# Output stores of 32 partitions joined in pairs to 64 partitions, in the last stage of a two-branch long convolution

## Chip, cores and metric

The kernel runs on one core of one Trainium2 chip. The metric is the device time of one execution in microseconds (us), lower is better. Before the change the median of three runs is 247.13 us (246.75 to 247.59).

## What is computed

The input is a sequence of 2048 positions with 448 channels in bfloat16. Two long convolutions over the positions are taken of it and mixed by a gate, position by position:

```python
g = sigmoid((x * gate_w).sum(-1, keepdims=True))          # x = A_u, (1, 2048, 448)
a = causal_conv(x, K) + x * Dskip      # K[d, l] = Re sum_n C exp(dt * A * l) * dt * B, by FFT
kv = short_conv4(k, shift_k) * v
b = x * (causal_conv(kv, ssm_k) + kv * ssm_D)              # by FFT
return g * a + (1 - g) * b                                # (1, 2048, 448)
```

The result is one array of 2048 x 448 bfloat16, that is 1,835,008 bytes.

## The kernel before, in words

**Layout.** Position t is written as 64 a + b, with a from 0 to 31 and b from 0 to 63, and the channel as 112 g + l, with g from 0 to 3. The work tiles hold (g, a) on the 128 partitions and (b, l) along each partition. The channels are worked through in four quarters H of 28 columns per group g (`NC`, line 25). `PLAN` (line 37) lists the steps: tables of the first convolution's kernel (T), the convolutions themselves (B, b, a, A), and the mixing of finished quarters (m). Each convolution is a chain of matmul stages with an elementwise product between them; their results leave PSUM by copies on VectorE or ScalarE, chosen one by one in `SIDES` (line 45).

**The last step.** The last entry of `PLAN` is the first convolution of quarter 3. Its last part is `end` (line 980). It runs over four pieces, h and k from 0 to 1, and each piece holds four of the sixteen values of y, where b = 16 x + y. For a piece it:

- collects the last matmul stage in a PSUM bank (lines 987 to 992),
- multiplies by the gate and adds the other branch on VectorE (lines 994 to 996),
- moves the data with matmuls in `relay` (line 965) from partitions (g, a) to partitions (x, a), so that all 448 channels of one position stand together,
- copies it with a change of sign into one of two row tiles, `lines[h]` (line 999; the other quarters have been put there already by `mix`, line 1071),
- stores the piece (lines 1000 and 1001).

**The stores.** After a piece is complete, partition 32 x + a of `lines[h]` holds 4 positions of 448 channels, 3584 bytes, which are contiguous in the output. The view `out_rows` (line 957) is the output as [x, a, y, l]; its x step is 16 positions and its a step is 64 positions. Line 1001 issues one transfer for each x: 32 partitions of 3584 bytes, 112 KB. x = 0 and 2 go to the queue of the sync engine (SP), x = 1 and 3 to that of ScalarE (ACT): `dmae` (line 770) lists the two. The four pieces make 16 transfers, and these are all the writes of the output.

**The order.** `Order` (line 132) records every call of the kernel and then issues the calls in the sequence that the string `ORDER` (line 51) gives; each instruction is chained behind the one before it on its engine. All records of the trace therefore carry line 144. The transfers that ScalarE issues stand in its own instruction stream, between its copies. Each transfer adds to one of eight completion counters used in turn, and waits until the transfer before it on the same counter has landed.

Of the kernel before, what the change touches and what calls it, by code (L numbers as in the profile page):

```python
# [110 lines left out]
)  # L111

def after(tc, ins, before):
# [55 lines left out]
def shaped(flat, shape, dtype=bf16, at=0):  # L169
    n = 1  # L170
    for s in shape:
        n *= s
    ap = flat if dtype is flat.dtype else flat.bitcast(dtype)
    ap = ap[:, at:at + n]
    names = "abcde"[:len(shape)]
    return ap.rearrange("p (%s) -> p %s" % (" ".join(names), " ".join(names)), **dict(zip(names, shape))) if len(shape) > 1 else ap
# [524 lines left out]
class Modes:  # L701
# [5 lines left out]
    def across(self, nm, put):  # L707
        for hf in range(2):
            for g in range(4):
                put(hf, g, self.raw[nm][:, g, hf * 128:(hf + 1) * 128])  # L710
# [36 lines left out]
def body(  # L747
# [22 lines left out]
    dmae = [nc.sync, nc.scalar]  # L770
# [143 lines left out]
    for b0 in range(0, 64, 8):  # L914
        pt = places.room()
        for i in range(2):
            for d in (0, -1, 1, -2, 2, -3, 3):
                t0 = b0 + 4 * i + d
                j0, j1 = max(0, -d), min(4, 4 - d)
                for g in range(4):  # L920
                    x = kT[g][:, t0 % 16, 2 + t0 // 16:2 + t0 // 16 + 4 * 31 + 1:4]
# [35 lines left out]
    out_rows = out[0].rearrange("(a x y) l -> x a y l", a=32, x=4)  # L957
    lines = []

    def line(y0):  # L960
        if not lines:
            lines.extend(qt([8, 448]) for _ in range(2))
        return lines[y0 // 8][:, y0 % 8:]

    def relay(o, g, part, first, last):
        for x in range(4):
            nc.tensor.matmul(o[32 * x:32 * x + 32].rearrange("p (y c) -> p y c", c=NC), lhsT=minus[:, 32 * g:32 * g + 32], rhs=part(x),
                             start=first, stop=last, tile_position=(0, 32 * x))

    def laid(t, H):  # L970
        return t.rearrange("p y (g h c) -> p h g y c", g=4, c=NC)[:, H]
# [8 lines left out]
    def end(U, H):  # L980
        across = lambda t, y0, n: t.rearrange("p (x y) c -> p x y c", x=4)[:, :, y0:y0 + n]
        for h in range(2):
            for k in range(2):
                ps, pt = (places.room()[:, 0] for _ in range(2))
                y0 = 8 * h + 4 * k
                b = across(ug[H], y0, 4)
                nc.tensor.matmul(ps[:, 0:448].rearrange("p (x y c) -> p x y c", x=4, c=NC), lhsT=minus[:], rhs=b, start=True, stop=False)
                for i in range(16):
                    for r in range(2):
                        l = 16 * (i // 4) + y0 + i % 4  # L990
                        nc.tensor.matmul(ps[:, i * NC:(i + 1) * NC], lhsT=G[:, l, r].rearrange("p g a -> p (g a)"), rhs=U[:, r, l],
                                         start=False, stop=(r == 1 and i == 15))
                t = shaped(arena["RK"][:], [4, 4, NC], at=448 * (2 * h + k))
                V.tensor_tensor(out=t, in0=ps[:, 0:448].rearrange("p (x y c) -> p x y c", x=4, c=NC),
                                in1=gt[:].rearrange("p (x y) -> p x y", x=4)[:, :, y0:y0 + 4].unsqueeze(3).to_broadcast([P, 4, 4, NC]), op=ALU.mult)
                V.tensor_tensor(out=t, in0=t, in1=b, op=ALU.add)
                for g in range(4):
                    relay(pt[:, 112 * g:112 * g + 112], g, lambda x: t[:, x], g == 0, g == 3)
                evac.minus(laid(line(y0)[:, 0:4], H), pt[:, 0:448].rearrange("p (g y c) -> p g y c", g=4, c=NC))
                for x in range(4):  # L1000
                    dmae[x % 2].dma_start(out_rows[x][:, y0:y0 + 4], lines[h][32 * x:32 * x + 32, 4 * k:4 * k + 4])

    held_open = []

# [50 lines left out]
    def conv_A(what, H, K):  # L1055
        X = spread_in(lambda c: uu[:, :, H * NC + c])
        transform(nc, places, W2, X, evac)
        X, S = swapped(X)
        if H < NQG - 1:
            transform(nc, places, W2, K, evac)  # L1060
            conv(products(nc, X, S, K), what, H)
            return
        U = qt([2, 64, NC])
        for c0 in (0, CB):
            transform(nc, places, W2, K, evac, c0, c0 + CB)
            for k0 in (0, 16):
                products(nc, X, S, K, k0, k0 + 16, c0, c0 + CB)
            stage_a(nc, places, R, whole(U, evac), (X, S), [range(c0, c0 + 8), range(c0 + 8, c0 + CB)])
        end(U, H)
# [57 lines left out]
```

## Time and profile before

| | |
|---|---|
| median of 3 runs | 247.13 us |
| the profiled execution's own time | 248.35 us |
| its span, first to last instruction | 246.4 us |
| busy: TensorE, VectorE, ScalarE | 85%, 93%, 89% of the span |
| bytes written to the device memory, whole run | 2.87 MB |
| first store of the output issued | 236.9 us |

The profile is one execution on the chip. Its span goes from the first instruction to the last; the execution's own time is 1.95 us longer than the span. Engines are PE (TensorE), DVE (VectorE), ACT (ScalarE), POOL (GpSimd) and SP (the sync engine); a name with a small q behind it (SPq, ACTq) is the engine's queue, where transfers are issued. The core has 16 DMA engines that carry out all transfers; the view of the transfers gives their mean busy share and the rate of bytes, and counts packets. In a row of the view by stretches of time stand the stretch, its length, the busy time of each engine with its instruction count, the granted clock of TensorE (PEclk), the busy share of the 16 DMA engines, and GB/s.

### The profile page before, as it was taken

The page shows a single profiled execution, that of the slowest core. Times are in us where ns is not written, and L with a number is a line of the kernel's source. Part 1 is how long each engine was busy: PE and PEld are TensorE (multiplying, and loading weights), DVE is VectorE, ACT ScalarE, POOL GpSimd, SP SyncE. Part 2 cuts the span into 40 slices and gives each one's busy share as a digit, 9 for nine tenths or more (in the row PEclk, how much of TensorE's full clock was granted, in tenths as well). Part 3 has the DMA queues.
Part 4 walks back from the last instruction along what each step waited for, and adds up shares of the span by engine and source line. Part 5 has one row for each costly group of instructions (what it writes and reads, how often), then busy time and mean ns, then how long its engine had stood idle before and what let it go on. Part 6 is the DMA issues. An engine that isn't in the chain of part 4 may idle for free.

```text
span 246.4 us, 12201 instructions
## 1 busy us (share of the span) xinstructions
PE 209.4 (85%) x5451; PEld 185.5 (75%) x5451; DVE 228.4 (93%) x394; ACT 220.4 (89%) x333; POOL 39.9 (16%) x112
## 2 busy tenths in 40 slices
PE   0747699877999998887899988979999999999970
PEld 0645277566988988787889977978989998998850
DVE  7999999999686999999999999999999999989870
ACT  5999999998999999999999999989999997586640
POOL 8700002030002141000011450001434102000000
PEclk9999799999999999999999999999999999999985
DMA  5997999993103498000688680000775402300035
GB/s 131 306 184 155 238 203 192 187 195 79 23 5 78 116 228 168 7 5 3 92 118 152 142 215 24 7 3 11 125 132 155 114 5 68 89 4 3 3 115 186
DMA packets 43347, 26.27 MB, mean 107 GB/s; under 512 B 34144, under 2 KB 40256, under 8 KB 43296
## 3 DMA queue, kind: packets, MB, share of 16 engines
q1 hardware_dynamic: 38848, 15.64, 30.9%
q0 software_dynamic: 3600, 8.95, 18.0%
q8 instruction: 42, 0.69, 1.2%
q10 hardware_dynamic: 848, 0.92, 1.1%
q14 instruction: 9, 0.07, 0.1%
HBM read 9.78 MB, written 2.87 MB: 51 GB/s over the span
## 4 chain that ended last, share of the span: by engine, by line
PE 36%; DVE 23%; ACT 19%; DMA 7%; issue 7%; SPq 4%; POOL 0%; DVEq 0%; ACTq 0%; POOLq 0%
PE ps L144 36%; ACT q L144 15%; DVE TP L144 10%; DVE TQ L144 5%; SPq L144 4%; DVE q L144 4%; ACT G L144 3%; DMA natu<-in_A_u_dram 3%; DMA gw<-in_gate_w_dram 2%; DMA TP<-TP 2%; DMA q<-in_B_ssm_k_dram 1%; DVE RK L144 1%; DVE ET L144 1%; DVE G L144 1%; DVE natv L144 1%
## 5 line engine op out<-in xcount | busy, mean ns | idle before, releaser
L144 ACT CAST q<-ps 128x896 bf16<-128x896 f32 (+4 forms) x172 | 133.2, 900 | 11.1 <-PE ps L144 10.6
L144 PEld LDWEIGHTS <-q 128*128 128x128 bf16 (+2 forms) x784 | 41.0, 134 | 8.9 <-issue 3.8
L144 PEld LDWEIGHTS <-G 128*128 128x128 bf16 (+2 forms) x1136 | 35.5, 103 | 15.3 <-issue 7.2
L144 DVE TENSOR_TENSOR TQ<-TQ,ET 128x896 bf16<-128x896 bf16 (+2 forms) x70 | 45.4, 682 | 0.1
L144 PE MATMUL ps<-q,s_W 128*128 128x112 bf16 (+1 forms) x544 | 33.5, 210 | 3.8 <-ACT q L144 2.1
L144 PE MATMUL ps<-sa_R,q 128*128 128x128 bf16 x448 | 33.6, 229 | 3.3 <-issue 1.7
L144 PE MATMUL ps<-TP,TQ 128*32 128x32 bf16 x1792 | 32.9, 240 | 2.1 <-issue 1.8
L144 PEld LDWEIGHTS <-s_W 128*128 128x128 bf16 x544 | 27.6, 97 | 7.6 <-issue 4.9
L144 PEld LDWEIGHTS <-TQ 128*32 128x32 bf16 x1792 | 29.9, 153 | 4.2 <-issue 2.3
L144 DVE TENSOR_TENSOR q<-q,q 128x3584 bf16<-128x3584 bf16 (+1 forms) x22 | 32.3, 1508 | 0.6 <-ACT q L144 0.6
L144 POOL DMA_DIRECT2D TP<-TP x15 | 13.4, 895 | 112.0 <-PE ps L144 64.8
L144 DVE TENSOR_TENSOR TP<-TP,ET 128x1792 bf16<-128x1792 bf16 (+3 forms) x25 | 31.5, 1269 | 0.1
L144 ACT ACTIVATE q<-hold 128x224 bf16<-128x224 f32 (+1 forms) x81 | 28.7, 410 | 0.1
L144 POOL DMA_DIRECT2D q<-q x30 | 16.1, 564 | 56.2 <-ACT q L144 30.2
L144 PEld LDWEIGHTS <-natu 128*64 128x64 bf16 (+1 forms) x288 | 21.5, 206 | 4.8 <-DMA natu<-in_B_k_dram 3.6
L144 PE MATMUL ps<-q,G 128*128 128x56 bf16 (+1 forms) x640 | 20.3, 182 | 1.0 <-ACT q L144 0.9
L144 ACT ACTIVATE ET<-q 128x1344 bf16<-128x1344 int16 (+1 forms) x12 | 17.3, 1477 | 0.0
L144 PE MATMUL ps<-Wc,natu 128*64 128x128 bf16 x224 | 16.5, 284 | 0.5 <-ACT q L144 0.5
L144 PE MATMUL ps<-Wc,natv 128*64 128x128 bf16 x224 | 16.1, 285 | 0.6 <-ACT q L144 0.6
L144 PEld LDWEIGHTS <-natv 128*64 128x64 bf16 x224 | 15.2, 213 | 1.5 <-issue 1.0
L144 DVE TENSOR_TENSOR TQ<-TQ 128x448 bf16<-128x448 bf16 (+2 forms) x35 | 15.3, 443 | 0.2
L144 PE MATMUL ps<-G 112*32 112x336 bf16 (+3 forms) x448 | 14.0, 274 | 1.3 <-issue 0.7
(96 smaller groups left out, 280.0 us busy)
## 6 DMA issues: line engine op xcount, KB each, us to landing
TP<-TP POOLq DMA_DIRECT2D x9, 448.0 KB, 5.8
q<-q SPq DMA_DIRECT2D x34, 112.0 KB, 3.4
q<-q POOLq DMA_DIRECT2D x30, 112.0 KB, 4.0
natu<-in_B_k_dram SPq DMA_DIRECT2D x2, 896.0 KB, 10.3
q<-in_B_ssm_k_dram SPq DMA_DIRECT2D x16, 112.0 KB, 3.8
natv<-in_B_v_dram SPq DMA_DIRECT2D x8, 224.0 KB, 5.3
natu<-in_A_u_dram SPq DMA_DIRECT2D x8, 224.0 KB, 8.1
TP<-TP POOLq DMA_DIRECT2D x6, 224.0 KB, 3.6
```

What stands on the lines that cost most here:

```text
L144: ins = f(*args, **kw)
```

## The change

In each piece, the four stores of 32 partitions become two of 64 partitions: x = 0 and 1 go in one transfer on SP's queue, x = 2 and 3 in one on ScalarE's. On the side of the output the transfer runs over 2 values of x, 32 values of a, and 1792 contiguous elements; on the side of the row tile it runs over 64 partitions and 1792 contiguous elements. The bytes, their places, and the instructions of PE, DVE and POOL stay as they are. The rest of the diff renumbers the calls in the string `ORDER`, since eight calls are gone; the order of the others is kept.

```diff
-                for x in range(4):
-                    dmae[x % 2].dma_start(out_rows[x][:, y0:y0 + 4], lines[h][32 * x:32 * x + 32, 4 * k:4 * k + 4])
+                for x in (0, 2):
+                    dmae[x // 2].dma_start(out_rows[x:x + 2, :, y0:y0 + 4], lines[h][32 * x:32 * x + 64, 4 * k:4 * k + 4])
```

In the built programs the instructions of the two queues differ only here (each line is output and source, and the extent of the output side):

```
SP   before: out<-q 32x1792   eight times      after: out<-q 2x32x1792   four times
ACT  before: out<-q 32x1792   eight times      after: out<-q 2x32x1792   four times
```

6 rows, old and new, of the table ORDER are left out of this document.

## Prediction

> **What bounds the kernel now.** The change touches only the stores of the output, so I read the end of the run: first the page's chain and its row of slices, then the view by stretches of time, the list of the queues' issues, and the transfers of the last 14.4 us.
>
> The chain of work that ended last, its final pieces (start, duration, what):
>
> ```profile
> 225.96 11.64 PE ps L144 x293
> ...
> 238.28 0.40 DVE RK L144
> 238.69 0.04 issue
> 238.73 0.89 PE ps L144 x28
> 239.62 0.02 issue
> 239.64 0.62 DVE q L144
> ```
>
> The last copy, on DVE, ends at 239.64 + 0.62 = 240.26 us. The span is 246.4 us (page, first line, below), so after the last computation about 6.1 us pass with nothing left but stores. What happens in them, by stretches:
>
> ```profile
> span 246.4 us, 12201 instructions
> ```
>
> ```profile
> 10.00:12.00 2.00, 1.34 (x15) 1.34 (x16) 2.00 (x10) 2.00 (x4) 1.38 (x14) 1.00 1.02 415
> 237.70:244.70 7.00, 0.86 (x32) 0.58 (x32) 1.86 (x4) 0.73 (x2) 0.00 (x0) 0.60 0.86 262
> 238.00:244.00 6.00, 0.86 (x32) 0.58 (x32) 1.56 (x4) 0.54 (x1) 0.00 (x0) 0.59 0.92 282
> 240.00:241.00 1.00, 0.00 (x0) 0.00 (x0) 0.26 (x1) 0.00 (x0) 0.00 (x0) 0.50 0.90 291
> 241.00:242.00 1.00, 0.00 (x0) 0.00 (x0) 0.00 (x0) 0.00 (x0) 0.00 (x0) 0.50 0.88 269
> 242.00:243.00 1.00, 0.00 (x0) 0.00 (x0) 0.00 (x0) 0.00 (x0) 0.00 (x0) 0.50 0.89 269
> 243.00:244.00 1.00, 0.00 (x0) 0.00 (x0) 0.00 (x0) 0.00 (x0) 0.00 (x0) 0.50 0.95 298
> 244.70:246.40 1.70, 0.00 (x0) 0.00 (x0) 0.00 (x0) 0.00 (x0) 0.00 (x0) 0.50 0.00 0
> ```
>
> The two columns to read are the last ones, the busy share of the 16 DMA engines and GB/s. From 238 to 244 us the engines are 92% busy at 282 GB/s; PE, DVE and ACT end in the meantime. After 244.7 us nothing moves, and 1.7 us later the span is over: that is the last completion and the program's end. **So the tail is bound by the DMA engines**, and they are what this change rearranges. The first row, from the loads at the start, is kept as the fastest rate of this trace: 415 GB/s with all engines busy.
>
> The stores themselves, as the trace lists them (count, issue times in ns, first and last start), and their queues in the stretch from 232 us on:
>
> ```profile
> L144 SPq DMA_DIRECT2D out_dram<-q x8: 315/362/558, 236.9 to 241.5; - x8
> L144 ACTq DMA_DIRECT2D out_dram<-q x8: 321/408/773, 236.9 to 242.1; - x8
> ```
>
> ```profile
> q1 hardware_dynamic: 384, 0.92, 23.9%
> q10 hardware_dynamic: 384, 0.92, 17.9%
> ...
> out_dram<-q SPq DMA_DIRECT2D x8, 112.0 KB, 3.0
> out_dram<-q ACTq DMA_DIRECT2D x8, 112.0 KB, 3.1
> ```
>
> q1 is SP's queue, q10 ACT's. Each queue's 8 stores have 8 x 32 = 256 rows of 3584 bytes, yet 384 packets: 16 more for each store. I read these as one completion packet from each of 16 engines, so each store of before lies on all 16, two rows on each. The packets took (0.239 + 0.179) x 16 engines x 14.4 us = 96.3 us, or 188 ns a row.
>
> **The change, part by part.**
>
> Removed: eight issues, four on SP and four on ACT, of 0.36 and 0.41 us. All issues of before are out by 242.1 + 0.77 = 242.9 us while the engines have work until 244.7, so fewer issues save at most the gaps of the engines, priced under the first rival. Removed too is a wait on reused completion counters: eight stores now have eight counters. In the waits of SP's queue it is small:
>
> ```profile
> SPq L144 <- DMA out_dram<-q: 0.4, 2, 0.2
> ```
>
> It lies under the full engines; I count it at nothing, and 0.4 us if that cover were gone.
>
> Moved: nothing. The programs stand in the same order on PE, DVE and POOL, and the eight remaining stores in the same places behind the same copies.
>
> Added: two kinds of thing, a longer issue and **another division over the DMA engines**.
>
> *Issue.* A store's description is longer. The nearest rows are SP's other 64-partition transfers and a transfer with only four rows (times in ns, as above):
>
> ```profile
> L144 SPq DMA_DIRECT2D q<-q x5: 461/548/1214, 202.8 to 209.2; - x5
> L144 SPq DMA_DIRECT2D d<-in_A_Dskip_dram x1: 864/864/864, 24.2 to 24.2; - x1
> ```
>
> I take 0.55 us, from the first of them because it too has 64 partitions: 0.2 us more than 0.362, which counts once, ahead of the first data. The ends are no change and 0.864 - 0.362 = 0.5 us. On ACT the copies stand behind the stores and would be late by as much; they stay hidden as long as the DMA engines have a backlog, and if that cover is gone they cost 0.2 us for each of the two pieces that ACT still copies after its first store.
>
> *Division.* This is the term that decides. Before, both sides of a store run over 32 in their outermost step. In the changed program the row tile's side runs over 64 partitions, but the output's side is 2 x 32 x 1792: its outermost step is x, with a count of 2. No transfer of the trace of before has an outermost count between 5 and 31, or one of 2; those of 32, 64, 112 and 128 are multiples of 16. So the division of a 2 x 32 store is not shown, and I bound it from both sides: over 16 engines as now, or by its outermost steps alone, one x per engine, 32 rows on each of 2 engines. The only row near to a short outermost count is the four-row one above, whose issue took 0.864 us, more than twice a store's; that says that a short count is handled otherwise, not how. I take 2 engines, since an equal deal of the outermost steps is the only one that all transfers of the trace have in common, and since a deal by rows would have to merge two steps (16 positions for x, 64 for a) that do not form one even stride. I also take it that both queues deal to the same two engines: each store of before starts its deal afresh over the same 16.
>
> The Trainium skill, page "DMA: Bandwidth & Descriptors", section "Why a DMA increments its semaphore by 16 and not by 1", states this rule: the number of engines is the largest up to 16 that divides the slowest dimension other than 1 of both access patterns, and SP's and ACT's transfers go to the lowest-numbered ones. By it, 2 and 64 give two engines, the same two for both queues. No run here shows that yet. Its section "Rules for kernel authors" speaks for the change instead (join small transfers, and do not cut by partition halves); by that advice alone the tail would only get shorter, as in the first rival.
>
> With two engines, each gets half of all rows: 512 / 2 = 256 rows of 3584 bytes. What a row takes on one engine:
>
> - 415 GB/s over 16 engines is 25.9 GB/s each, so 138 ns a row, the low end;
> - 188 ns by the packets of the tail;
> - 282 GB/s over 16 engines is 17.6 GB/s each, so 203 ns a row with gaps, the high end.
>
> The slower figures come from 16 engines at 282 GB/s together; two at 25.9 would move 52 GB/s, so what holds back the sixteen has little hold on two. I therefore stay near the row with 415 GB/s and take 145 ns: 256 x 0.145 = 37.1 us. The ends are 35.3 us and 52.0 us.
>
> Do the two engines ever run dry? The first pair of stores alone gives each engine 64 rows, 64 x 0.145 = 9.3 us of work, beyond the last issue of before at 242.9 us. So they do not, and a piece that comes later costs nothing. If a queue took no second store before its first had gone out, each later pair would add a gap, 3 x about 1.4 us (0.55 us of issue and about 0.8 us from an issue to first data, 236.9 to 237.7); the high end covers that.
>
> **Sum.** First data 237.7 + 0.2, rows 37.1, last completion and end 1.7: the span becomes 276.7 us, 30.3 more than 246.4. Against the profiled execution's own time that is 248.35 + 30.3 = 278.7; that execution was 1.2 us above the median of the runs shown, and on the median it is 247.13 + 30.3 = 277.4 us. With the ends of the row's time: 237.7 + 35.3 + 1.7 = 274.7, so 275.4 on the median; 237.9 + 52.0 + 1.7 = 291.6, so 292.3.
>
> **Rivals.**
>
> *All 16 engines still share each store (faster).* The mechanism is at the same place, the engines in the tail. If the deal is by rows after all, every engine gets four rows of each store where it had two, with half the completions. The idle shares in the rows from 240 to 244 us add up to 0.10 + 0.12 + 0.11 + 0.05 = 0.38 us, and 0.08 x 6 = 0.5 us from 238 to 244; closing these gaps gives 246.6 us. If the rate rose to the 415 GB/s of the loads, 1.835 MB would take 4.4 us in place of 7.0, 2.6 us less: 244.5 us. The longer issue, 0.2 us, stands against it; 244.5 to 247.3. It decides as soon as the number of engines stays at 16. For it speaks that the engines are at 88 to 90% while stores are still being issued; against it the outermost count of 2.
>
> *Two engines for each queue, not the same ones (slower by less).* If ACT's and SP's stores lay on different pairs, each engine would have 128 rows: 128 x 0.145 = 18.6 us, span 237.9 + 18.6 + 1.7 = 258.2, time 258.9 us. Against it stands that every store of before, on either queue, has 16 completions, so that both queues reach the same engines and no engine is set aside for one.
>
> *The change doesn't do what it says.* If each joined store were cut into two of 32 rows again further down, engines and rate would be as before: 247.1 us.
>
> **How the numbers follow.** Two shared engines 0.88, all sixteen 0.07, two pairs 0.04, cut again 0.01. The predicted time is that of the first, 277.4 us. Its own ends are 275.4 and 292.3; below, I allow 2 us for a row faster than any stretch here shows on average, since two engines meet less company: 273 to 292.5. That interval holds about 0.95 of the first case, 0.84 in all, so it need not reach the rivals. A measurement of this kernel can tell a change from none at about 0.3%, 0.7 us. The sixteen-engine case is faster by more than that in about 0.05 and within it in 0.02; the cut stores are within it, 0.01. So: faster 0.05, within 0.03, slower 0.92.
>
> **What would show it.** In the profile after, the chain up to 240 us and the busy times of PE, DVE and ACT should be unchanged. From 238 us on the DMA share should sit near 2/16 = 0.125 for some 37 us at about 50 GB/s, where it was 0.92 at 282. Each queue's packets in the tail should be 4 x (64 + 2) = 264 if two engines post a completion, 4 x (64 + 16) = 320 if sixteen do. The time from issue to landing, 3.0 us before, should grow store by store to over 25 us for the last. The forecast is wrong if the share in the tail is near 0.9 (first rival) or near 0.25 (second). If the share is 0.125 but the tail lasts beyond 45 us, only the time of a row was wrong.

## The result, and the profile after

The changed kernel takes 277.97 us, the median of 6 runs (277.35 to 279.34); the kernel before took 247.15 us in 6 runs beside it. The ratio is 1.1255, with a 95% interval of 1.122 to 1.1289: **slower by 12.6%, 30.8 us.** The forecast was 277.4 us, in a range of 273 to 292.5.

The profiled execution took 277.35 us, its span is 275.6 us. The engines' busy times are those of before to 0.3 us (PE 209.2 for 209.4, DVE 228.4 and ACT 220.4 unchanged), so the time is not in the computation. The chain of work that ended last stops, as before, with a copy on DVE (start, duration, what):

```profile
237.66 0.62 DVE q L144
```

That copy ends at 238.28 us, and then 37.3 us pass to the end of the span, where 6.1 us passed before. What fills them is seen in the stretches of the changed kernel (stretch, length, busy engines, PEclk, share of the 16 DMA engines, GB/s):

```profile
236.30:241.30 5.00, 0.73 (x32) 0.47 (x32) 1.43 (x4) 1.09 (x2) 0.00 (x0) 0.61 0.13 33
241.30:273.90 32.60, 0.00 (x0) 0.00 (x0) 0.00 (x0) 0.00 (x0) 0.00 (x0) 0.50 0.13 52
273.90:275.60 1.70, 0.00 (x0) 0.00 (x0) 0.00 (x0) 0.00 (x0) 0.00 (x0) 0.50 0.00 0
```

The share of 0.13 is 2 engines of 16. For 37.6 us two engines are busy and fourteen are idle, at 33 GB/s for the first 5 us and then at 52, where the tail of before had 282 at a share of 0.92. The queues from 232 us on, and the stores as the trace lists them (issue times in ns):

```profile
q1 hardware_dynamic: 264, 0.92, 5.7%
q10 hardware_dynamic: 264, 0.92, 5.2%
```

```profile
L144 SPq DMA_DIRECT2D out_dram<-q x4: 536/1048/2346, 235.1 to 239.9; - x4
L144 ACTq DMA_DIRECT2D out_dram<-q x4: 527/1353/1607, 235.1 to 240.0; - x4
```

The bytes of a queue are the same 0.92 MB, but its packets are 264 = 4 x (64 + 2): two completion packets a store, where there were 16. The program's end now waits 31.9 us for the last store, where before its longest wait for a store was 2.7 us (us in total, times, longest); the wait on reused counters is gone:

```profile
SPq L1122 <- DMA out_dram<-q: 31.9, 1, 31.9
```

One number needs care. In this profile the first store is issued at 235.1 us, in that of before at 236.9, though the programs are alike up to there; over the eight experiments below it lies between 235.9 and 238.7. I take that as scatter of the stages ahead, and compare tails by **the time from the first store's issue to the span's end**: 246.4 - 236.9 = 9.5 us before, 275.6 - 235.1 = 40.5 us after, 31.0 us more.

### The profile page after: what moved, and what is told of

Same layout as the page of the kernel before. It is cut to its first block, busy times and chain, and to the rows that moved or that the text cites. A ratio compares the mean times of both kernels' runs of the same rounds, so it can differ in the third digit from the quotient of the medians.

```text
span 275.6 us, 12190 instructions
## 1 busy us (share of the span) xinstructions
PE 209.2 (76%) x5451; PEld 185.8 (67%) x5451; DVE 228.4 (83%) x394; ACT 220.4 (80%) x333; POOL 39.9 (14%) x112
## 3 DMA queue, kind: packets, MB, share of 16 engines
q0 software_dynamic: 3600, 8.95, 15.8%
## 4 chain that ended last, share of the span: by engine, by line
ACT 30%; PE 25%; DVE 19%; issue 7%; DMA 4%; POOL 1%; DVEq 0%; SPq 0%; ACTq 0%; POOLq 0%
PE ps L144 25%; ACT q L144 24%; DVE TP L144 5%; DVE q L144 4%; DVE TQ L144 3%; DVE natv L144 3%; DMA q<-q 2%; ACT ET L144 2%; DMA natv<-in_B_v_dram 2%; ACT G L144 1%; POOL q L144 1%; DVE ET L144 1%; DVE G L144 1%; ACT RK L144 1%; DVE RK L144 1%
## 5 line engine op out<-in xcount | busy, mean ns | idle before, releaser
L144 PEld LDWEIGHTS <-q 128*128 128x128 bf16 (+2 forms) x784 | 41.8, 135 | 9.7 <-issue 5.3
```

What stands on the lines that cost most here:

```text
L144: ins = f(*args, **kw)
```

## Experiments

Theory A is that of the prediction: the DMA engines are dealt out by the outermost count, and both queues get the same ones. Theory B is the rival that the profile of after does not exclude alone: a joined store is slow as such (64 partitions, twice the rows in one issue, a longer issue). All eight kernels keep the computation (the last takes its pieces in another order). Four of them (64 even rows, 2 x 16, 8 x 8 and 16 x 4 rows) write rows to other places of the output than the kernel should; the bytes and the length of each contiguous run stay as they are. Ratios are to the kernel before, run beside them: 248.05 us beside the runs with 64 even rows, 4 x 32 rows, half of the change and joining along the row, 248.46 beside the other four. That is about 1 us more than beside the result, so a ratio says more than a time here.

### Joined stores with 64 even rows

```diff
+    out_even = out[0].rearrange("(p y) l -> p y l", y=16)
-    dmae[x // 2].dma_start(out_rows[x:x + 2, :, y0:y0 + 4], lines[h][32 * x:32 * x + 64, 4 * k:4 * k + 4])
+    dmae[x // 2].dma_start(out_even[32 * x:32 * x + 64, y0:y0 + 4], lines[h][32 * x:32 * x + 64, 4 * k:4 * k + 4])
```

> The joined stores keep their 64 partitions, their 224 KB and their places in the two queues, but the output side now runs over 64 rows in one even step of 16 positions, so its outermost count is 64 in place of 2. The rows land at other positions of the output than they should; the bytes and the length of each contiguous run are the same. Theory A, the DMA engines are dealt out by the outermost count: all 16 engines again, 4 x (64 + 16) = 320 packets for each queue in the tail, a busy share near 0.9 there, and 244.5 to 247.3 us, likeliest 246.6. Theory B, the cost lies in a joined store as such (64 partitions, twice the rows in one issue, the longer issue on its queue): about 278 us, as with the change.

Measured: 248.58 us, ratio 1.0035 (1.0008 to 1.0061). SP's queue in the tail (ACT's has 320 packets too), its stores, and the stretch from first to last row:

```profile
q1 hardware_dynamic: 320, 0.92, 5.9%
```

```profile
L144 SPq DMA_DIRECT2D out_dram<-q x4: 466/497/537, 238.4 to 241.8; - x4
```

```profile
239.60:246.20 6.60, 0.68 (x32) 0.47 (x32) 1.47 (x4) 0.54 (x1) 0.00 (x0) 0.72 0.88 276
```

With the same 64 partitions and 224 KB in one issue, 30 us are gone as soon as the outermost count is 64. Theory B falls. The size of A's forecast was off, however: I had this form at 244.5 to 247.3 us where before took 247.1, and it is no faster than before. The rows take 6.6 us in place of 7.0, but the first rows come 239.6 - 238.4 = 1.2 us after the first issue, where before it was 237.7 - 236.9 = 0.8. From the first issue to the end it is 247.9 - 238.4 = 9.5 us, as before. So joining itself, on all 16 engines, is worth nothing here.

### Sixteen separate stores with an outermost count of 2

```diff
-    for x in (0, 2):
-        dmae[x // 2].dma_start(out_rows[x:x + 2, :, y0:y0 + 4], lines[h][32 * x:32 * x + 64, 4 * k:4 * k + 4])
+    for x in range(4):
+        dmae[x % 2].dma_start(out_rows[x // 2 * 2:x // 2 * 2 + 2, x % 2 * 16:x % 2 * 16 + 16, y0:y0 + 4],
+                              lines[h][32 * x:32 * x + 32, 4 * k:4 * k + 4])
```

> The joining is undone and the short outermost count kept: sixteen stores of 32 partitions and 112 KB, as before the change, but the output side of each runs over 2 x 16 rows (16 rows of one x, 16 of the next). The rows of a pair land exchanged in part; bytes and run lengths are the same. Theory A: two engines for every store, 8 x (32 + 2) = 272 packets for each queue, 52 GB/s, the same 256 rows for each of two engines as with the change: 276 to 282 us, the upper part if the second eight stores wait for the counters of the first. Theory B, the joined store as such is the cost: about 247 us as before.

Measured: 278.48 us, ratio 1.1208 (1.1154 to 1.1262). SP's queue in the tail (ACT's has 272 packets too), and a stretch of it:

```profile
q1 hardware_dynamic: 272, 0.92, 4.5%
```

```profile
245.00:265.00 20.00, 0.00 (x0) 0.00 (x0) 0.00 (x0) 0.00 (x0) 0.00 (x0) 0.50 0.13 52
```

The stores are as many and as large as before the change, and the loss is there in full: 272 = 8 x (32 + 2). Together with the run above this separates the two parts of the change. **The joining costs next to nothing (0.35% above), the outermost count of 2 costs the rest.** Later stores did wait for earlier ones to land, 15.8 us in four waits on SP, but the two engines had work all the while (0.13 in the stretch above):

```profile
SPq L144 <- DMA out_dram<-q: 15.8, 4, 7.5
```

### Other outermost counts: 4, 8, 16

One store of 128 partitions for each piece, 4 x 32 rows:

```diff
+    dmae[1 - h].dma_start(out_rows[:, :, y0:y0 + 4], lines[h][:, 4 * k:4 * k + 4])
```

> One store of 128 partitions for each piece, 4 x 32 x 1792 on the output side, two pieces on each queue; correct output. Theory A: an outermost count of 4 gives four engines, the same four for both queues, so 512 / 4 = 128 rows on each at the 137 ns a row that the changed kernel shows, 17.5 us of stores: 257 to 259 us, and 2 x (128 + 4) = 264 packets for each queue. Theory B: still more rows in one issue, so 278 us or more.

Joined stores of 64 partitions over 8 x 8 and over 16 x 4 rows:

```diff
+    out_dealt = out[0].rearrange("(h j i y) l -> h i j y l", h=2, j=8, i=8)      # or j=4, i=16
-    dmae[x // 2].dma_start(out_rows[x:x + 2, :, y0:y0 + 4], lines[h][32 * x:32 * x + 64, 4 * k:4 * k + 4])
+    dmae[x // 2].dma_start(out_dealt[x // 2][:, :, y0:y0 + 4], lines[h][32 * x:32 * x + 64, 4 * k:4 * k + 4])
```

> Joined stores of 64 partitions, but the output side runs over 8 x 8 rows, outermost count 8 (the rows land in another order; bytes and run lengths are the same). Theory A: eight engines, 4 x (64 + 8) = 288 packets for each queue, 64 rows on each at 137 ns, 8.8 us, and 2 to 4 us of a slow start as the store of four engines had (21.5 us from first to last row where 17.5 were worked out): 12 us of rows, 252 to 255 us. A rule by which only a count of 16 or more is dealt out, and any shorter one goes to two engines, would give 278.

> As the run with 8 x 8 rows, but 16 x 4, outermost count 16 (the rows land in another order). Theory A: sixteen engines, 320 packets for each queue, the time of the run with 64 even rows, 248 to 249.5 us, though the output side is still described by two row steps. If it was the second row step on the output side, not the count, that cost the time: 278.

Measured: 261.88 us for 4, the median of three runs (a fourth took 264.95), ratio 1.0573 (1.0529 to 1.0616); 254.53 us for 8, ratio 1.0252 (1.0193 to 1.0311); 248.86 us for 16, ratio 1.0014 (0.9986 to 1.0042). SP's queue in the tail and a stretch with the queues full, for 4, then 8, then 16:

```profile
q1 hardware_dynamic: 264, 0.92, 5.4%
```

```profile
245.00:255.00 10.00, 0.00 (x0) 0.00 (x0) 0.00 (x0) 0.00 (x0) 0.00 (x0) 0.50 0.26 105
```

```profile
q1 hardware_dynamic: 288, 0.92, 5.5%
```

```profile
244.50:248.00 3.50, 0.00 (x0) 0.00 (x0) 0.00 (x0) 0.00 (x0) 0.00 (x0) 0.50 0.51 202
```

```profile
q1 hardware_dynamic: 320, 0.92, 5.9%
```

```profile
239.00:245.00 6.00, 0.68 (x32) 0.47 (x32) 0.87 (x2) 0.54 (x1) 0.00 (x0) 0.71 0.84 282
```

The packets are 2 x (128 + 4), 4 x (64 + 8) and 4 x (64 + 16), the shares 4/16 and 8/16, and the rate goes with them: 52, 105 and 202 GB/s for 2, 4 and 8 engines, 25 to 26 for each. Sixteen do not reach 16 x 26 = 416 with these stores; here they stop at 282, as before. The last of the three also rules out that the second row step on the output side was the cost: 16 x 4 has one too, and lies 0.14% above before, not told apart from it. The rows of four engines took 21.5 us, 4 us longer than worked out; the last section has what is known of it. All counts tried are powers of two, so rules that differ only at other counts are not told apart.

The rule cited from the Trainium skill ("DMA: Bandwidth & Descriptors", "Why a DMA increments its semaphore by 16 and not by 1") agrees with all of these: counts of 2, 4, 8, 16 and 64 beside 32, 64 or 128 partitions gave 2, 4, 8, 16 and 16 completions. Which of the sixteen engines they are, no run here shows.

### Whose engines: half of the change, and one queue

Only SP's stores joined:

```diff
+    dmae[0].dma_start(out_rows[0:2, :, y0:y0 + 4], lines[h][0:64, 4 * k:4 * k + 4])
+    for x in (2, 3):
+        dmae[1].dma_start(out_rows[x][:, y0:y0 + 4], lines[h][32 * x:32 * x + 32, 4 * k:4 * k + 4])
```

> Only SP's half of the change: x = 0 and 1 joined on SP, x = 2 and 3 as two stores of 32 partitions on ACT's queue. Theory A: two engines have 4 x 32 = 128 rows of the joined stores and 2 of each of the 8 others, 16, so 144 rows at 137 ns, 19.7 us of stores: 259 to 261 us; ACT's stores land late too, since each has two of its rows on the two loaded engines. Theory B: SP's queue has the same four joined stores as with the change; if they are slow by themselves, each at its queue's pace, the end stays near 277 us.

All eight joined stores on SP's queue:

```diff
-    dmae[x // 2].dma_start(out_rows[x:x + 2, :, y0:y0 + 4], lines[h][32 * x:32 * x + 64, 4 * k:4 * k + 4])
+    dmae[0].dma_start(out_rows[x:x + 2, :, y0:y0 + 4], lines[h][32 * x:32 * x + 64, 4 * k:4 * k + 4])
```

> The changed kernel with all eight joined stores on SP's queue, none on ACT's; correct output. If both queues deal to the same two engines, nothing is lost by this: 512 rows over two engines at 137 ns, 35 us, and 277 to 281 us as with the change; q1 alone has 8 x (64 + 2) = 528 packets. If each queue had two engines of its own, one queue would take twice as long as the two: near 312 us.

Measured: 264.24 us for the half, ratio 1.068 (1.0644 to 1.0716); 278.18 us for one queue, ratio 1.1192 (1.1143 to 1.1242). In the run with one queue:

```profile
q1 hardware_dynamic: 528, 1.84, 8.8%
```

```profile
245.00:265.00 20.00, 0.00 (x0) 0.00 (x0) 0.00 (x0) 0.00 (x0) 0.00 (x0) 0.50 0.13 53
```

One queue alone moves the same 53 GB/s as the two did together (52), and the time is the same, so both had been filling the same two engines; a second queue adds nothing. The half shows the neighbours' side. ACT's eight stores were unchanged, with 16 engines each, and yet landed in a median of 6.4 us where before it was 3.1. That fits rows of theirs standing in line on the two loaded engines. ACT's own copy then came late: the issue of a store ahead of it took 1.91 us (chain of the run with the half; below it the wait that the trace names):

```profile
240.46 1.91 ACTq L144
242.37 0.05 issue
242.41 0.54 ACT q L144
```

```profile
242.41 0.54 ACT L144 ACTIVATE q<-ps 128x448 bf16<-128x448 f32 x1 [2.35 <-DMA out_dram<-q]
```

I had 259 to 261 us for this run; it took 3 us more. Its last 8 us, from 254 to 262, run at the full 52 GB/s, so the 3 us were lost before. There lie ACT's held queue and the slow first rows of the last section, both left out by the estimate of 144 rows; which of them cost how much was not shown.

### Joined along the row instead

The two pieces of one half are taken one after the other and stored together, 32 partitions of 7168 bytes:

```diff
-    for h in range(2):
-        for k in range(2):
+            for h, k in ((0, 0), (1, 1), (1, 0), (0, 1)):
...
+                if h != k:
+                    continue
+                for i, x in enumerate((2, 1, 0, 3)):
+                    dmae[i % 2].dma_start(out_rows[x][:, 8 * h:8 * h + 8], lines[h][32 * x:32 * x + 32])
```

> Eight stores of 224 KB, as many as with the change, but joined along the row in place of the partitions: 32 partitions of 7168 bytes, outermost count 32. For this the two pieces of one half are taken one after the other, and the half is stored after its second piece. Correct output. Theory A: 16 engines; the first half's stores start about 1 us later than the first stores of before, the second half's at the same time as before; the rest is 0.92 MB at 282 to 415 GB/s, 3.3 to 2.2 us, from about 241.1 or from where the first half ends: 245 to 247.3 us. Theory B: eight large transfers, four on each queue, cost what those of the change cost: about 278 us.

Measured: 249.06 us, ratio 1.0049 (1.0022 to 1.0076). Issues and the stretch of the rows:

```profile
L144 SPq DMA_DIRECT2D out_dram<-q x4: 315/336/357, 237.0 to 240.2; - x4
```

```profile
237.80:244.80 7.00, 0.68 (x32) 0.47 (x32) 1.42 (x4) 0.55 (x1) 0.00 (x0) 0.75 0.91 262
```

Eight stores of 224 KB on 16 engines, with issues as short as before, take the same 7.0 us at 262 GB/s as sixteen of 112 KB. From the first issue to the end it is 246.7 - 237.0 = 9.7 us. I had 245 to 247.3 us, up to 2.1 us less than before; there is no gain, it is 0.5% slower. Neither this form nor the even rows beat the kernel before, so a kernel that brings the even rows to their proper places promises no gain; none was run.

## Why the prediction was right, point by point

- **What bounds the end.** The tail of the DMA engines; right. Computation is unchanged, the whole loss lies behind the first store: 31.0 us of the tail, 30.8 us in the medians.
- **Division over two engines.** Right, and shown: a share of 0.13, two completions a store, and the loss follows the outermost count alone, with joining (the change) and without (sixteen stores of 2 x 16). Three readings on the way to it were off. The trace of before was not silent on short counts: besides `d`, the transfer `dB` has four rows too (issue 0.958 us), and SP's queue has 1528 packets of 4 bytes in the whole trace for its 97 transfers, which is 95 x 16 + 2 x 4. That fits four completions for each of these two, so four engines were to be read there. And the length of an issue, which the prediction takes from `d`, does not tell a short count: stores of 16 x 4 rows on all 16 engines have a median issue of 0.59 us on SP, more than the shortest of 2 x 32 rows on two, 0.54. Nor does the section "Rules for kernel authors" of the Trainium skill's page "DMA: Bandwidth & Descriptors" speak only for the change, as the prediction has it: that holds of the two rows that it takes up, while the row "Use all 16 engines" says that an outermost dimension below 16 confines a transfer to at most that many engines, and the runs with counts of 2, 4 and 8 agree with it.
- **The same two for both queues.** Right: one queue alone takes the same time. The rival of two pairs, 258.9 us, is excluded with it.
- **Time of a row.** I took 145 ns, between 138 and 203, near the loads' rate. The full stretch, 52 GB/s, is 26 GB/s for each engine, and 3584 bytes / 26 = 138 ns: the low end. But the first 5 us ran at 33 GB/s. Together 37.6 us, 37.1 forecast. That the two agree to 0.5 us is in part luck: the 7 ns on top of the low end, 1.8 us over 256 rows, stood in for a slow start of about 2.3 us that I had not named.
- **First data.** Forecast 0.2 us later than before; it came 236.3 - 235.1 = 1.2 us after the issue where it was 0.8, so 0.4 later. The end, 1.7 us, was right.
- **Issue.** I took 0.55 us; the shortest are 0.527 and 0.536, right for a free queue. But the median is 1.0 on SP and 1.4 on ACT; issues got longer while the two engines were behind (last section). The case for which I had allowed a gap (no second store taken before the first has gone) did not arise: the share is 0.13 in both stretches of the tail. The cover held.
- **Sum.** From first issue to end, 276.7 - 236.9 = 39.8 forecast, 40.5 measured. The span came out 1.1 us below the forecast only because this execution reached the first store 1.8 us earlier.
- **First rival.** Its condition did not hold in this kernel, and its price was wrong too: with all 16 engines kept, the joined form has ratios of 1.0035 and 1.0014, where 246.6 on 247.13 would be 0.998. The idle 0.4 to 0.5 us of the engines was closed in part (6.6 us of rows for 7.0) and given back before the first row (1.2 us for 0.8); the rate of the loads was not reached, at any size or number of stores.

## What to carry to other kernels

Before joining transfers, look at the outermost count of both sides as the instruction carries it. Here counts of 2, 4 and 8 on the output side meant 2, 4 and 8 DMA engines of 16, in stores of 112, 224 and 448 KB. Count completion packets for each transfer, and compare the DMA share with n/16; both show it at a glance. In this tail, bound by the rate of all engines, joining stores that already use all of them gained nothing (ratios 1.0014 to 1.0049). And stores confined to two engines also delayed full stores of another queue, from 3.1 to 6.4 us in the median.

## What the runs showed of the hardware that was not expected

- **A slow start.** In the changed kernel 33 GB/s were moved in the first 5 us of rows, then 52. With four engines it was 49 GB/s, then 105. With all joined stores on one queue there is one stretch at 25 GB/s (four engines, then one queue):

```profile
237.20:242.00 4.80, 0.68 (x32) 0.48 (x32) 1.44 (x4) 0.54 (x1) 0.00 (x0) 0.63 0.24 49
240.70:242.70 2.00, 0.00 (x0) 0.00 (x0) 0.00 (x0) 0.00 (x0) 0.00 (x0) 0.50 0.09 25
```

  Two things come together. Rows take longer: in the changed kernel SP's 42 rows between 236.3 and 241.3 us have a share of 11.6% of 16 engines, so 221 ns each, and the four engines count as busy at 0.24 of 0.25. And the engines can stand idle: 0.09 of 0.125 in the run with one queue. The computation alone is not the reason, since it ends at 238.3 us in the changed kernel. There ACT's first rows move only from 241.3 us on, 6.2 us after their issue and 5 us after SP's. What slows the first rows, and why the second queue waits, was not tried.
- **Long issues while the engines are behind.** With all joined stores on one queue an issue took up to 4.3 us. Two engines need 32 x 138 ns = 4.4 us for the 64 rows of one store, so it looks as if an issue waits until as much has gone out; that was not tried:

```profile
L144 SPq DMA_DIRECT2D out_dram<-q x8: 543/3126/4307, 237.5 to 255.9; - x8
```

- **Sixteen engines do not add up.** 2, 4 and 8 engines gave 25 to 26 GB/s each for these stores. Sixteen gave 262 to 282 GB/s over the stretches shown, 16 to 18 each, in stores of 112 KB and of 224 KB, of 3584 and of 7168 byte rows. The best 5 us of the run with 64 even rows had 315, 20 each, still below the 415 of the loads:

```profile
240.50:245.50 5.00, 0.41 (x28) 0.21 (x15) 0.62 (x1) 0.54 (x1) 0.00 (x0) 0.69 0.94 315
```

  What holds sixteen back was not identified.
